# Keeping one step's split weights on chip between the two halves of an attention and gated-MLP layer, with key weights in two pieces and a new order

## The chip, the cores and the metric

The kernel runs on one core of one Trainium2 chip. The core has a matrix engine (TensorE, PE in the profile, with its weight loads as PEld), a vector engine (DVE), a scalar engine (ACT), a general engine (POOL) and SyncE (SP), which here only issues DMA transfers. The metric is the device time of one execution in microseconds. For the kernel before, three runs gave 565.55, 566.1 and 568.32 us; the median is 566.1.

## The reference

For x of 2048 tokens by 512, normalised to `xn` (layer norm without weights):

```python
qkv = xn @ wqkv                                   # 32 heads of 16
pq, pk = q @ w_phi, k @ w_phi                     # per head, 16 by 16
phi(p) = concat(softmax(p), softmax(-p))
kv = sum over tokens of phi_k^T v;  z = sum over tokens of phi_k
s = (phi_q kv / (phi_q z + 1e-6)) @ wo            # all tokens, no mask
h = (gate * (gate > 0)) * up;  gate = xn @ W_gate, up = xn @ W_up     # 512 x 1376 each
out = x + s * silu(h @ W_down)
```

All inputs and the output are fp32.

## The kernel before, in words

**Precision and tiles.** Every large product is made of three fp32r matmuls: each operand is split into a high part (a rounding copy on ACT) and a low part (the difference, on DVE or POOL). Gate and up are computed together with a scheme of seven products of sums of blocks (Winograd's) instead of eight, so that each step has seven groups of six matmuls. The hidden width of 1376 is padded to 11 steps of 128 (`NF` = 11, f = 0 to 10).

**Halves.** The tokens go in two halves of 1024. The first half is in one long list, `ORDER`: it loads and normalises all 16 token blocks, folds `w_phi` into the key and query weights, forms keys, values and queries and the sums `kv` and `z`, and then makes the 11 gate/up steps of the first half, most of its down products and the first three pairs of query blocks. Each name in `ORDER` is a small operation; `Plan.run` issues them in the order of the list, and each engine works off its own instructions in that order. The names used below:

- `ldN`, `bnN`, `pwN`, `biN`, `apN`, `TN`: load, statistics, root, shift, scaling and turning of token block N (tiles `xt`, `pxT`); `lcb` loads constants (`cb`), `lkN` a piece of the key weights (`wkT`), `FkN` folds a quarter of them on PE (`pfold`, two passes for each of four products); `pk` is the key product that follows.
- `rwF` loads the raw gate and up weights of step F (`rawg`, from `wf`), `rdF` the down weights (`rawd`). `fsF` and `ftF` form sums on POOL (`tab`). `faF`, `fbF`, `fcF`, `fdF`, `feF` are the rounding copies on ACT into `wa`, `wb`, `wc`, `wd`, `fd`, and `falF`, `fblF` and so on the differences on POOL.
- `putwaF` and the like store these split weights to DRAM (`ws`): nine transfers of 256 KB for a step, two each for `wa`, `wb`, `wc` and `fd` and one for `wd`.
- `gF.0` to `gF.6` are the seven products of step F on PE (`ga`, `seed`, `gc`, `gd`); `gtF`, `gmF`, `geF` and so on are their sums on ACT and DVE; `haF` to `hdF` split the result into `hh`.
- `dnCJI` is a down product on PE for chunk C of steps, half-block J and rows I (`py`), `dyCJI` adds it up (for the first chunk a copy on ACT, `y<-py`).
- `of_K` loads output weights (`wor`).

After the list, still in the first half, the last chunk of the down product, the SiLU, and the output product (`pso`) with the split attention result (`oh`, `ol`, in `o_split`, from `of`) follow. The second half is a loop over f in which `gate_up` uses weights that `f_reload` fetches from `ws`; part 0 brings `wa` and `wb`, part 1 `wc`, `wd` and `fd`. Its order on the engines is set when the program is built, by a planner with costs and due times (`Clock`) and by the order of the code.

**Order and buffers.** All loads and stores of SP go through one queue in the order of issue; an issue waits until the transfer eight before it has landed. Buffers come from pools with a fixed number: 24 of 4 KB for each partition (`u4`: a pair such as `wa`, `fd` or `hh`, or `oh`, `ol`), 14 of 2 KB (`u2`, among them `wd`). A tile that is made when no buffer is free waits for the last reader of an old one.

At the end of the first half the code fetches the weights of step 0 and, in the output products, the first part of step 1:

```python
        last_split()
        drain()
        if half == 0:
            f_reload(0, 0)
            f_reload(0, 1)
        fs = CHUNKS[-1]
```

All instructions that pass through `InOrder` carry its one line in the profile: 129 before, 132 after.

Of the kernel before, what the change touches and what calls it, by code (L numbers as in the profile page):

```python
# [42 lines left out]
td2 bi4 pw6 pk3.1 td4 sm0 bi6 sq2.1 ap4 pq1.1 pk2.3 ep7 pv0.1 sps1 tl1.0 sm1 sc0 T4 spill0 th2.0 pw7 sc1 st8 bi7
z0 sums2 ph0 mx2 th2.1 lo5 ap7 tl1.1 pl0 pk3.2 q1.0 pk3.3 q2.0 hS2 pv1.0 hi4 sh2 lo4 st10 pq1.0 ex2 mx3 ap6 P1.2
ep10 pv1.1 slo2 tl2.0 T6 sm2 pq2.0 pv0.2 th3.0 sh3 pv1.2 sc2 cS2 th3.1 tl2.1 ex3 hi6 P6.2 ph1 pv3.0 ep8 z1 pv2.0
sm3 tl3.0 tl3.1 pv1.3 pl1 cU2 pv3.1 pv2.1 sc3 T7 sq1.0 vh1 vl1 lo6 P7.2 st11 pw8 th4.0 th4.1 P5.2 z3 tl4.0 sums3
lpm pv3.2 cW2 pv0.3 aw2 hi7 tl4.1 hS3 bi8 ap8 lo7 vh0 P2.2 bankd P3.2 pw10 bi10 slo3 vl0 bankc st9 pv3.3 au2
bankb ap10 vh3 spill2 banka mx4 ep11 kv0 P4.2 ep9 pv2.2 pw9 ph3 vl3 sh4 st13 ex4 pl3 kv1 pv2.3 vh2 mx5 q3.0 ph2
z2 sh5 ex5 ep13 vl2 sm4 pw11 pq3.0 sm5 bi9 P1.3 pw13 kv3 pl2 cS3 sq1.1 vh4 T8 sc5 P6.3 spill3 ld12 ap9 sc4 hi8
z5 bi13 P3.3 cU3 lo8 bi11 T9 P7.3 kv2 sums4 ph5 cW3 P4.3 hi9 vl4 mx6 hS4 pl5 sh6 lo9 ph4 mx7 q3.1 spS2 spill1  # L50
slo4 sh7 z4 ex6 ap11 P1.4 pq3.1 vh5 sm6 cS4 P5.3 aw3 ex7 sm7 sc6 vl5 pl4 st15 P6.4 cU4 vh7 P3.4 P2.3 sc7 ap13
au3 P7.4 vl7 cW4 T10 T11 hi10 hi11 kv4 mx8 ph6 lo10 sums5 P4.4 kv5 st12 P5.4 ph7 z6 hS5 lo11 pl6 q4.0 ep12 sh8
aw4 mx9 ex8 pl7 ep15 P2.4 sh9 pw12 pq4.0 ld14 kv7 ex9 sq3.1 au4 vh6 P1.5 q4.1 bi12 sm8 slo5 vl6 ap12 sm9 cS5
P6.5 z7 st14 kv6 sc8 pq4.1 T12 sc9 cU5 T13 P7.5 hi12 z8 ph8 sums6 lo12 cW5 pl8 hS6 hi13 P3.5 slo6 vh8 ep14 mx10
P4.5 spS3 q5.0 lo13 q5.1 z9 ph9 pq5.0 pw14 P1.6 vl8 mx11 kv8 sh11 sh10 ex11 vh9 pq5.1 pw15 sm11 sq5.1 bi15 sc11
ex10 pl9 cS6 bi14 P5.5 rw0 sm10 sq4.0 P6.6 z11 ph11 P3.6 aw5 sc10 ap14 P2.5 vh11 ap15 mx12 T15 cU6 fd0 hi15 pl11
sq2.0 P7.6 vl9 sq3.0 cW6 au5 vl11 lo15 T14 kv9 sums7 kv11 sq5.0 sh12 ph10 hi14 P4.6 lo14 mx13 q6.1 vh10 z10 fdl0
ex12 pl10 P1.7 hS7 vl10 sh13 slo7 rd0 pq6.1 sm12 kv10 sc12 P5.6 fs0 cS7 ex13 P3.7 ph12 rw1 P6.7 aw6 fa1 ft0 cU7
fa0 sm13 fs1 sq4.1 sc13 mx14 P2.6 P7.7 rd1 q6.0 z13 cW7 vh13 ft1 sh14 fal1 fal0 fb0 putwd0 au6 pq6.0 vl13 P5.7
ph13 rw2 P4.7 ex14 aw7 pl13 vh15 mx15 rd2 q8.1 vh12 sm14 P2.7 pq8.1 sh15 sc14 kv13 fc0 q7.0 fb1 ex15 au7 sm15  # L60
vl12 fbl0 vl15 pl12 sq6.1 sq6.0 q8.0 sc15 ql0.1 ph15 pq7.0 g0.0 kv12 g0.1 sq8.1 pq8.0 qt0.1 fcl0 qm0.1 q7.1 pl15
rw3 vh14 z15 fe0 fd1 fbl1 ph14 gt0 qs0.1 g0.2 pl14 fe1 vl14 gm0 fdl1 kv15 pq7.1 g0.3 qe0.1 kv14 fc1 sq8.0 ka fa2
sq7.1 ge0 fel0 gf0 kb g0.4 g0.5 fs2 z14 g0.6 ft2 kp2 fb2 gp0 g1.0 ql2.0 fc2 ql0.0 fcl1 gt1 fs3 putwa0 kp3 qt0.0
z12 qm0.0 qs0.0 gs0 gn0 g1.1 ft3 gg0 g1.2 rd3 fd2 kt2 fel1 kp0 sq7.0 gm1 ge1 kt0 g1.3 kh2_ ha0 hc0 ql1.0 fa3
putwc0 gf1 g1.4 kh0_ kl0_ g1.5 kl2_ rw4 fbl2 fal2 qe0.0 g1.6 fb3 fc3 zp1 kt3 fcl2 qt2.0 g2.0 g2.1 gp1 qa0.0
ql1.1 zc1 fd3 gn1 putwd1 fdl2 rd4 zp0 gg1 hd0 g2.2 fs4 gs1 qm2.0 hb0 putwd2 kh3_ qs2.0 ha1 hb1 gt2 gm2 hc1
putwb1 zc0 g2.3 ge2 fbl3 qt1.1 gf2 putwb0 qm1.1 qa0.1 g2.4 kl3_ fal3 gp2 g2.5 ft4 kp1 g2.6 qs1.1 putwc1 rw5 kt1
kh1_ gn2 putwb2 dn010 g3.0 g3.1 qt1.0 kl1_ fdl3 hd1 qm1.0 putwa2 gt3 fcl3 gs2 dn013 g3.2 putwc3 putwa1 qw0.1 gm3
dy010 of_1 putfe0 putwb3 qb0.1 qw0.0 fc4 fcl4 putwa3 qe1.1 gg2 ge3 fd4 fb4 qs1.0 dn012 g3.3 qb0.0 gf3 fa4 dy012
fal4 fdl4 g3.4 putwc2 oh_1 dn000 dy000 g3.5 ql2.1 dn011 fs5 dy013 ha2 gp3 ft5 qr0 ow_1 g3.6 fe3 gs3 fd5 ha3 qd0  # L70
qn0.0 fbl4 qn0.1 qx0.10 dn002 fa5 dy011 qe2.0 fel3 g4.0 hb3 dn001 qx0.00 dy002 putwc4 qh0.10 gn3 rd5 qx0.11
qo0.10 gt4 putwd3 rw6 qw1.1 hb2 fdl5 qh0.11 qh0.00 qe1.0 qx0.01 qh0.01 g4.1 qo0.11 g4.2 dn003 os_1 qo0.00 gm4
qo0.01 g4.3 qk0.11 fal5 putwd4 dy001 qk0.00 rd6 ge4 fb5 dy003 gg3 putfe1 rw7 fc5 qw1.0 qa1.0 of_2 g4.4 qa1.1 hc3
fe2 putwa5 qk0.01 gf4 g4.5 fbl5 fel2 gp4 qc0.00 putwa4 qk0.10 qb1.1 g4.6 sf0 fs7 qc0.11 gs4 fcl5 qb1.0 dn110
putwd5 gn4 qr1 fd7 g5.0 rd7 dn113 qc0.10 g5.1 hd3 qt2.1 fd6 qd1 gg4 sg0 putwb4 sl0 dy113 hc2 gt5 putwc5 g5.2 hd2
qn1.0 gm5 qc0.01 dy110 ge5 dn112 fa6 fs6 rw8 putfe3 oh_2 g5.3 fa7 fal6 ft6 ft7 qn1.1 qz0.0 gf5 dn111 dy111 fb6
g5.4 dy112 gp5 qz0.1 fc6 qm2.1 g5.5 fb7 dn101 fbl6 qx1.00 fdl6 gs5 sw0 g5.6 fal7 dn100 qs2.1 putwb5 gn5 g6.0 gg5
ow_2 fe5 dy101 fcl6 qx1.10 dn102 fbl7 qh1.00 qx1.01 fe4 gt6 hc4 dy102 rd8 g6.1 putwb6 qh1.01 qh1.10 qo1.00 fdl7
dn103 hd4 qo1.01 gm6 putwa7 qe2.1 qo1.10 qx1.11 g6.2 qk1.01 ge6 fa8 fel4 qw2.1 g6.3 qh1.11 fel5 putwd7 qc1.01
sf1 g6.4 dy103 qw2.0 hc5 qa2.0 hd5 qk1.00 of_3 putwd6 g6.5 putwa6 qb2.1 putfe2 gf6 fc7 os_2 qo1.11 g6.6 qa2.1  # L80
putwc6 g7.0 fs8 gp6 ol0 qk1.11 sg1 putfe5 gs6 qc1.00 g7.1 fcl7 qc1.11 gt7 qb2.0 fe6 gn6 qk1.10 fal8 fel6 qc1.10
g7.2 putwb7 gm7 gg6 qr2 dn203 g7.3 ge7 fd8 oh_3 qd2 g7.4 rw9 gf7 ft8 qn2.0 putfe4 sl1 dy100 dn200 qn2.1 qz1.1
g7.5 gp7 gs7 dn202 rd9 fb8 putwc7 dy200 fe7 putwa8 qx2.00 qx2.11 ha4 fc8 fs9 fa9 g7.6 qh2.00 g8.0 ha5 fbl8 ow_3
dy203 gn7 gt8 g8.1 fdl8 g8.2 gm8 fcl8 dy202 g8.3 ge8 g8.4 qx2.10 ft9 sw1 qo2.00 rw10 fc9 gg7 g8.5 qx2.01 os_3
qh2.01 dn201 hb4 oa0 gf8 g8.6 fa10 fal9 fel7 qo2.01 qh2.10 qo2.10 gp8 qz1.0 fcl9 fb9 qk2.00 dy201 fd9 fbl9 g9.0
hb5 qh2.11 qo2.11 fs10 g9.1 qk2.11 qc2.00 g9.2 gt9 gn8 putwc8 fdl9 hc7 hc6 qk2.01 hd7 hd6 gs8 putwb9 gm9 of_0
ha6 qc2.11 fal10 putwa9 ge9 qk2.10 ft10 g9.3 qc2.01 g9.4 putwd8 dn211 gf9 oh_0 g9.5 dy211 dn210 qc2.10 ow_0
# [1433 lines left out]
```

## Time and profile before

| what | value |
|---|---|
| runs, us | 565.55, 566.1, 568.32 |
| profiled execution, own time | 568.91 us |
| its span, first to last instruction | 567.1 us |
| PE busy | 554.2 us (98%) |
| DVE, ACT, POOL busy | 415.0, 290.7, 423.5 us |
| moved by DMA | 136.14 MB, mean 240 GB/s |
| mean granted clock of TensorE | 0.996 |

The span is told from one profiled execution; the runs' times are of whole executions. A share of busy time is a mean over very different stages, so the stages are read one by one. In rows of instructions the columns are start, duration, engine, line, operation, tile written and tiles read, and in brackets how long the engine stood idle and what ended that.

### The profile page before, as it was taken

The numbers are of one execution on the slowest core, as the hardware profiler recorded it, in microseconds if no ns is written. First come the engines' busy times: TensorE is split into PE (matmuls) and PEld (weight loads), VectorE is DVE, ScalarE is ACT, GpSimd is POOL, SyncE is SP. The second block draws the span as 40 slices with busy tenths as digits, with TensorE's granted clock in tenths as the row PEclk, the third lists the DMA queues.
The fourth block names the chain that finished last, engine by engine and source line by source line (L and its number), as shares of the span: only waits on it lengthen the run. The fifth ranks groups of instructions, "written<-read, shape, count | busy, mean of one in ns | idle before, by whom it ended". The sixth has DMA issues, their size and how long they took to land.

```text
span 567.1 us, 8003 instructions
## 1 busy us (share of the span) xinstructions
PE 554.2 (98%) x2618; PEld 463.0 (82%) x2618; DVE 415.0 (73%) x621; ACT 290.7 (51%) x517; POOL 423.5 (75%) x325
## 2 busy tenths in 40 slices
PE   7999999999999999999899999999999999999997
PEld 6888888888888788878688887888888888888886
DVE  4998899889748899879664532599995959774322
ACT  4998887766565366445243232224563544534610
POOL 1798777688998898889886705553878888888476
PEclk8999999999999999999999999999999999999999
DMA  8646935375746888978999999996665766649883
GB/s 280 263 149 168 260 75 149 75 205 148 205 142 173 304 314 305 314 267 289 348 265 277 362 420 375 390 374 253 188 195 186 233 203 205 204 126 319 220 251 125
DMA packets 81562, 136.14 MB, mean 240 GB/s; under 512 B 7408, under 2 KB 34416, under 8 KB 80624
## 3 DMA queue, kind: packets, MB, share of 16 engines
q1 hardware_dynamic: 77920, 122.97, 63.2%
q0 software_dynamic: 3456, 12.58, 11.3%
q8 instruction: 21, 0.34, 0.3%
q14 instruction: 21, 0.17, 0.1%
q10 hardware_dynamic: 144, 0.07, 0.0%
HBM read 73.47 MB, written 53.74 MB: 224 GB/s over the span
## 4 chain that ended last, share of the span: by engine, by line
PE 86%; DMA 5%; POOL 4%; issue 2%; ACT 1%; DVE 1%; SPq 1%; ACTq 0%; POOLq 0%; DVEq 0%
PE py L129 17%; PE seed L129 9%; PE pd L129 8%; PE pa L129 8%; PE pso L129 8%; PE pq L129 8%; PE pc L129 5%; PE gc L129 4%; PE gd L129 3%; PE ga L129 3%; PE pkv L129 3%; PE pnum L129 2%; PE pk L129 2%; PE pv L129 2%; PE pfold L129 2%
## 5 line engine op out<-in xcount | busy, mean ns | idle before, releaser
L129 PE MATMUL py<-fd,hh 128*128 128x512 f32 x528 | 130.1, 389 | 0.0
L129 PEld LDWEIGHTS py<-fd,hh 128*128 128x128 f32 x528 | 99.0, 188 | 20.5
L129 DVE TENSOR_TENSOR y<-py,y 128x512 f32<-128x512 f32 x40 | 27.2, 687 | 32.1 <-PE py L129 32.1
L129 POOL TENSOR_TENSOR phl<-ek,phl 128x1024 fp32r<-128x1024 f32 x16 | 39.3, 2454 | 7.2 <-ACT phl L129 7.0
L129 PE MATMUL pso<-wo,oh 128*128 128x512 f32 (+1 forms) x136 | 39.8, 377 | 0.0
L129 POOL TENSOR_TENSOR ez<-eq,zB 128x1024 f32<-128x1024 f32 x16 | 38.5, 2415 | 1.1 <-PE py L129 1.1
L129 POOL TENSOR_TENSOR ol<-of,oh 128x1024 fp32r<-128x1024 f32 x8 | 19.1, 2399 | 25.8 <-issue 16.8
L129 PE MATMUL ga<-XT,wa 128*128 128x512 f32 x132 | 34.2, 394 | 0.0
L129 PE MATMUL pa<-XT,wa 128*128 128x512 f32 x132 | 33.7, 389 | 0.0
L129 PE MATMUL seed<-XT,wb 128*128 128x512 f32 x132 | 33.7, 390 | 0.0
L129 POOL TENSOR_TENSOR hh<-e,hh 128x512 fp32r<-128x512 f32 x11 | 14.3, 1296 | 25.7 <-ACT hh L129 25.7
L129 POOL TENSOR_TENSOR y<-y,ys 128x512 f32<-128x512 f32 x24 | 30.8, 1290 | 0.9 <-ACT ys L129 0.5
L129 DVE TENSOR_TENSOR y<-pso,y 128x512 f32<-128x512 f32 (+1 forms) x15 | 9.8, 656 | 29.2 <-PE pso L129 29.2
L129 PEld LDWEIGHTS ga<-XT,wa 128*128 128x128 f32 x132 | 24.5, 188 | 5.4 <-issue 0.5
L129 PEld LDWEIGHTS pa<-XT,wa 128*128 128x128 f32 x132 | 24.7, 188 | 5.1
L129 PEld LDWEIGHTS pso<-wo,oh 128*128 128x128 f32 x136 | 25.0, 188 | 4.7
L129 PEld LDWEIGHTS seed<-XT,wb 128*128 128x128 f32 x132 | 24.6, 188 | 5.0
L129 PE MATMUL pso<-wo,ol 128*128 128x512 f32 (+1 forms) x68 | 25.7, 378 | 1.2 <-POOL ol L129 1.2
L129 ACT ACTIVATE eq<-pnum 128x512 f32<-128x512 f32 x32 | 17.8, 592 | 15.8 <-PE pnum L129 15.8
L129 POOL TENSOR_TENSOR y<-y,sx 128x512 f32<-128x512 f32 x13 | 16.7, 1333 | 11.6 <-DMA sx<-x 10.5
L129 ACT ACTIVATE hh<-e 128x512 fp32r<-128x512 f32 x11 | 7.0, 633 | 33.6 <-DVE e L129 33.6
L129 POOL TENSOR_TENSOR pTl<-ez,pTh 128x1024 fp32r<-128x1024 f32 x10 | 24.1, 2406 | 0.0
(239 smaller groups left out, 1639.6 us busy)
## 6 DMA issues: line engine op xcount, KB each, us to landing
zacc<-ek POOLq DMA_DIRECT2D x16, 512.0 KB, 4.6
XT<-xts SPq DMA_DIRECT2D x7, 1024.0 KB, 14.5
rawg<-wf SPq DMA_DIRECT2D x11, 512.0 KB, 4.5
ws<-wa SPq DMA_DIRECT2D x22, 256.0 KB, 5.9
ws<-wc SPq DMA_DIRECT2D x22, 256.0 KB, 5.1
ws<-wb SPq DMA_DIRECT2D x22, 256.0 KB, 4.5
...
```

The lines of the kernel that those rows point to most:

```text
L129: return self.tc.keep_in_program_order(op(*a, **k))
```

## The change

Three things change.

1. Step 10 (`KEPT`) is not stored: `putwa10`, `putwb10`, `putwc10`, `putwd10` and `putfe10` go, and its split weights stay in their buffers. The second half takes the steps in the order 10, 0, 1, ..., 9 (`STEPS`), its down chunks are (10, 0), (1, 2), (3, 4), (5, 6), (7, 8, 9), and the reload of step 0 at the end of the first half goes; the one of the first part of step 1 in the output products becomes that of step 0. Nine stores and nine loads fewer.
2. The key weights are loaded in two pieces of 512 KB instead of four of 256 KB.
3. `ORDER` is a new list of the same operations, but for those that went.

```diff
+KEPT = NF - 1
+STEPS = [KEPT, *range(NF - 1)]
+CHUNKS_2 = [(10, 0), (1, 2), (3, 4), (5, 6), (7, 8, 9)]
 ORDER = """
-ld0 ld1 ld5 bn0 pw0 bn1 lcb lk0 st5 ap0 pw1 lk1 T0 bi1 Fk0 Fk1 ld2 ap1 T1 lk2 bn2 hi0 lo0 kh0 lk3 Fk2 kc0 lq0
+lcb ld1 bn1 pw1 lk0 ld0 Fk0 bi1 ap1 bn0 kh0 T1 Fk1 lk1 ld3 kl0 pw0 Fk2 lq0 ap0 hi1 lo1 kc0 lv0 kh1 Fk3 kc1 kc2
...
@@ prep_ops
                 if i is None and f in CHUNKS[-1]:
                     WD[f] = T[name]
+                elif i is not None and f == KEPT:
+                    FT.setdefault(f, [None] * 4)[i] = T[name]
...
+        if f == KEPT:
+            return
         for name, i in ((wa, 0), (wb, 2), (wc, 4), (fd, 7)):
             store(name, i, True)
@@ load_ops
-        for k in range(KD):
-            raw(f"lk{k}", "wkr", lambda: u8((P, KD, D), "wkT"), slice(k, k + 1), wkT[:, k:k + 1, :])
         for k in range(2):
+            raw(f"lk{k}", "wkr", lambda: u8((P, KD, D), "wkT"), slice(2 * k, 2 * k + 2), wkT[:, 2 * k:2 * k + 2, :])
@@ the halves
-        for f in range(NF) if half else ():
-            if f == 0:
+        for n, f in enumerate(STEPS if half else ()):
+            after = STEPS[n + 1] if n + 1 < NF else None
+            if n == 0:
                 queries = pace.add(all_queries(1), 5)
-            if f + 1 < NF and f + 1 not in FT:
-                f_reload(f + 1, 0)
+            if after is not None and after not in FT:
+                f_reload(after, 0)
...
-            run(gate_up(f, f > 1, lambda: f + 1 < NF and f_reload(f + 1, 1)))
-            for c, fs in enumerate(CHUNKS[:-1]):
+            run(gate_up(f, n > 1, lambda: after is not None and f_reload(after, 1)))
+            for c, fs in enumerate(CHUNKS_2[:-1]):
...
-        if half == 0:
-            f_reload(0, 0)
-            f_reload(0, 1)
-        fs = CHUNKS[-1]
+        fs = (CHUNKS_2 if half else CHUNKS)[-1]
...
-            HS.pop(g), WD.pop(g)
+            HS.pop(g)
+            if half or g != KEPT:
+                WD.pop(g)
...
             if half == 0 and m == 1:
-                f_reload(1, 0)
+                f_reload(STEPS[1], 0)
```

**The first instructions.** On SP, the first issues of the program before (`xt` are token blocks, `cb` the constants, `wkT` key weights):

```order
L129 DMA xt<-x 128x512 x3
L129 DMA cb<-cst 128x512
L129 DMA wkT<-wkT 128x512 x2
L129 DMA xt<-x 128x512
L129 DMA wkT<-wkT 128x512 x2
L129 DMA wqT<-wqT 128x1024
```

On SP after the change; the numbers at the end are the tile's shape, so `wkT` now moves 512 KB at a time, and one token block stands ahead of the key weights instead of three:

```order
L132 DMA cb<-cst 128x512
L132 DMA xt<-x 128x512
L132 DMA wkT<-wkT 128x1024
L132 DMA xt<-x 128x512
L132 DMA wkT<-wkT 128x1024
L132 DMA xt<-x 128x512
L132 DMA wqT<-wqT 128x1024
```

On PE before, behind the dummy products on `idle` (`pxT` turns a token block, `pfold` folds weights):

```order
L129 MATMUL pidle<-idle 128x128 x8
L129 MATMUL pxT<-ident,xt 128x128 x4
L129 MATMUL pfold<-cb,wkT 128x128 x8
L129 MATMUL pxT<-ident,xt 128x128 x4
L129 MATMUL pfold<-cb,wkT 128x128 x8
L129 MATMUL pk_304<-B11h,XT 128x512
```

On PE after the change; the first fold now stands ahead of the first turned block, and both turned blocks ahead of `pk`:

```order
L132 MATMUL pidle<-idle 128x128 x8
L132 MATMUL pfold<-cb,wkT 128x128 x4
L132 MATMUL pxT<-ident,xt 128x128 x4
L132 MATMUL pfold<-cb,wkT 128x128 x12
L132 MATMUL pxT<-ident,xt 128x128 x4
L132 MATMUL pk_302<-B11h,XT 128x512
```

**The first down products.** On ACT in the gate/up steps of the first half, around the first copies of down products (`y<-py`) before:

```order
L129 ACTIVATE XT<-pkb 128x2x64
L129 ACTIVATE t<-ga 128x512
L129 ACTIVATE y<-py 128x512
L129 ACTIVATE wc<-tab 128x512
L129 ACTIVATE eq<-eq 128x32x16 x2
L129 ACTIVATE wd<-rawg 128x256
L129 ACTIVATE wb<-tab 128x512
L129 ACTIVATE wa<-rawg 128x512
L129 ACTIVATE y<-py 128x512
L129 ACTIVATE woh<-wor 128x512
L129 ACTIVATE y<-py 128x512 x2
```

On ACT at the same place after the change. `wd<-rawg` is `fd6`, which reads the seventh load of gate weights; before it, `wd<-rawg` read the fifth, and one `y<-py` stood ahead of it; now two `y<-py` stand right behind it:

```order
L132 ACTIVATE t<-ga 128x512
L132 ACTIVATE wb<-tab 128x512
L132 ACTIVATE hh<-m 128x512
L132 ACTIVATE fd<-rawd 128x512
L132 ACTIVATE y<-py 128x512
L132 ACTIVATE eq<-eq 128x32x16 x2
L132 ACTIVATE wd<-rawg 128x256
L132 ACTIVATE y<-py 128x512 x2
L132 ACTIVATE sh<-sums 128x1024
L132 ACTIVATE wa<-rawg 128x512
```

On SP before, the rows that end in the seventh `rawg` load (`ws` are stores of split weights, `pql` query loads):

```order
L129 DMA ws_0_105<-wa 128x512
L129 DMA ws_1_106<-wa 128x512
L129 DMA ws_4_100<-wc 128x512
L129 DMA ws_5_101<-wc 128x512
L129 DMA pql<-pq_76 128x2x256
L129 DMA ws_4_118<-wc 128x512
L129 DMA ws_5_119<-wc 128x512
L129 DMA rawd<-wf 128x512
L129 DMA ws_6_111<-wd 128x512
L129 DMA rawg<-wf 128x1024
```

On SP after the change, the rows that end in it; a pair of output-weight loads (`wor`) and seven stores now stand close ahead:

```order
L132 DMA wor<-wo 64x1x512 x2
L132 DMA ws_6_120<-wd 128x512
L132 DMA ws_2_89<-wb 128x512
L132 DMA ws_3_90<-wb 128x512
L132 DMA rawd<-wf 128x512
L132 DMA ws_0_87<-wa 128x512
L132 DMA ws_1_88<-wa 128x512
L132 DMA ws_2_80<-wb 128x512
L132 DMA ws_3_81<-wb 128x512
L132 DMA rawg<-wf 128x1024
```

**The end of the first half.** On SP before, behind the reload of the operands of the second half (`XT`), the last of 20 stores and then the loads of step 0, ahead of the tokens `sx` for the output:

```order
L129 DMA ws_8_140<-fd 128x512
L129 DMA ws_0_168<-wa 128x512
L129 DMA ws_1_169<-wa 128x512
L129 DMA ws_7_148<-fd 128x512
L129 DMA ws_8_149<-fd 128x512
L129 DMA ws_6_174<-wd 128x512
L129 DMA ws_7_166<-fd 128x512
L129 DMA ws_8_167<-fd 128x512
L129 DMA wa<-ws_0_78 128x512
L129 DMA wa<-ws_1_79 128x512
L129 DMA wb<-ws_2_80 128x512
L129 DMA wb<-ws_3_81 128x512
```

On SP after the change, at the same place; no store and no load of weights stands between `XT` and `sx`, and step 0 comes behind the second `sx`:

```order
L132 DMA XT<-xts 128x2048 x7
L132 DMA sx<-x 128x512 x4
L132 DMA yk_177<-y 128x512
L132 DMA yk_178<-y 128x512
L132 DMA sx<-x 128x512 x2
L132 DMA wa<-ws_0_78 128x512
L132 DMA wa<-ws_1_79 128x512
L132 DMA wb<-ws_2_80 128x512
L132 DMA wb<-ws_3_81 128x512
L132 DMA out<-y 128x512 x6
```

More of the change, by code (lines that the diff above doesn't have):

```diff
@@ L43 @@
[L43 to L87, printed above, removed]
@@ new lines @@
+T0 kh2 lq1 bn3 hi0 kh3 ld2 pw3 lv1 pk1.0 kl1 Fq0 bi3 pk1.1 kc3 kl2 vh_0 ap3 qh0 ld5 Fq1 td1 pk1.2 sums0 Fq2 kl3
+vh_1 qh1 vl_0 ld4 lo0 vh_2 ld12 ql0 bn2 vl_1 qh2 ql1 pw2 T3 pk1.3 vl_2 hi3 lo3 st4 bi2 ap2 pk0.0 ld13 Fq3 qh3
+td3 pv1.0 pk0.1 ql2 st5 pk3.0 ld6 pv1.1 T2 ld11 hi2 mx1 ep4 pk0.2 pv1.2 sh1 th3.0 ql3 pk3.1 sps0 ld7 pw4 ep5
+vh_3 st7 pk0.3 lo2 bi4 ld9 pw5 tl3.0 sums1 ap4 vl_3 th1.0 ex1 q1.0 tl1.0 pv1.3 ep7 mx0 bi5 sh0 q1.1 pq1.0 ld8
+th1.1 ex0 st6 sm1 pw7 sm0 ep6 pq1.1 T4 vh1 td2 sc0 ap5 tl1.1 vl1 pw6 z0 pk3.2 sps1 q2.0 T5 bi7 sc1 hi4 pk2.0
@@ new lines @@
+sm4 sh5 P5.2 cS3 sc4 P3.3 aw2 sq3.0 ex5 ap9 st12 sm5 pl3 P6.3 spill2 ld14 z4 P2.2 sc5 pw10 T9 cU3 ap8 kv2 hi9
+au2 vh4 ph4 T8 P7.3 ep12 bi10 kv3 cW3 lo9 sums4 vl4 P5.3 hi8 hS4 mx6 P4.3 ph5 lo8 ap10 pl4 aw3 P2.3 slo4 st13
+kv4 sh6 mx7 au3 ex6 P1.4 sh7 vh5 pw12 z5 cS4 q3.1 sm6 ex7 pl5 sc6 ld15 st15 sm7 ep13 pq3.1 vl5 P6.4 cU4 ph6 P3.4
+T10 P7.4 hi10 pw13 sc7 lo10 T11 cW4 bi13 sums5 z6 mx8 hi11 kv5 P4.4 vh6 hS5 q4.1 pl6 lo11 ph7 vl6 mx9 ap13 z7
+bi12 q4.0 pq4.1 pl7 P5.4 sq2.1 sh8 sh9 kv6 ex8 slo5 sm8 pq4.0 aw4 P1.5 P2.4 ex9 ap12 ep15 sc8 vh7 cS5 ph8 P6.5
@@ new lines @@
+P3.5 sm9 z8 cU5 au4 T12 sc9 st14 spS2 pw15 hi12 mx10 vl7 pl8 P7.5 lpm T13 z9 vh9 cW5 ep14 kv7 lo12 sums6 vh8
+P4.5 vl8 bi15 ph9 hi13 q5.0 pl9 sh10 lo13 ex10 P5.5 mx11 hS6 kv8 sm10 pq5.0 aw5 vl9 pw14 sh11 sc10 vh11 P1.6
+slo6 spill3 cS6 spS3 ex11 P2.5 vl11 ph10 kv9 ap15 rw0 bi14 P6.6 au5 q5.1 z10 sm11 sq4.0 vh10 rd0 ap14 sc11 vl10
+pl10 cU6 fd0 T14 pq5.1 P7.6 sq5.1 T15 hi14 sums7 ph11 cW6 P3.6 hS7 sq5.0 kv10 z11 rw1 hi15 P4.6 pl11 lo14 lo15
+q6.1 slo7 fdl0 mx13 pq6.1 P1.7 mx12 sq3.1 P5.6 sh13 sq6.1 fs0 cS7 fs1 sh12 ex13 sq4.1 aw6 kv11 P6.7 rd1 sm13
@@ L93 @@
+putwa8 putfe7 hd7 g10.0 putwc9 gn9 dn313 qz2.1 putwb9 qz2.0 g10.1 ha8 fcl10 ow_0 fd10 gt10 wl1 dn303 gm10 fdl10
+g10.2 wl3 oa1 ge10 g10.3 dy303 hc8 ha9 gf10 hb8 ol2 os_2 hb9 g10.4 gg9 os_0 putfe6 putfe9 wl2 putfe8 ql3.1 gp10
+dn301 wl0 dy301 xrA11 gs10 g10.5 hc9 oa2 dn310 dy311 dy310 hd8 xrS2 xrA12 g10.6 dn312 gn10 xrS3 gg10 dy312 dn300
+fel10 xrS1 dy300 dy313 ha10 hd9 xrA22 xrS4 dn302 hb10 hc10 hd10 dy302
 """
```

46 lines of the change are left out of this document (36 added, 10 removed).

## The prediction

> **What bounds the kernel now.** I read the page's first lines, then the busy time by stretch, then who TensorE (PE) waited for, then the timelines at those places.
>
> ```profile
> span 567.1 us, 8003 instructions
> PE 554.2 (98%) x2618; PEld 463.0 (82%) x2618; DVE 415.0 (73%) x621; ACT 290.7 (51%) x517; POOL 423.5 (75%) x325
> ```
>
> PE is busy for 554.2 of 567.1 us and runs at full clock nearly throughout. Both programs list the same matmuls, so the change can win or lose only in the 12.9 us in which PE is not busy, and in its slow start. Where those are:
>
> ```profile
> core 0: us, PE busy (x) PEld busy (x) DVE busy (x) ACT busy (x) POOL busy (x), PEclk, DMA share, GB/s
> 0.00:10.00 10.00, 6.02 (x24) 4.78 (x25) 3.27 (x11) 4.00 (x7) 1.55 (x6) 1.00 0.77 224
> 10.00:20.00 10.00, 10.00 (x66) 9.56 (x66) 7.68 (x19) 7.40 (x14) 3.98 (x4) 0.83 1.03 409
> 190.00:200.00 10.00, 9.23 (x43) 7.38 (x42) 9.03 (x15) 1.08 (x4) 9.92 (x10) 1.00 0.95 327
> 250.00:260.00 10.00, 9.17 (x44) 7.29 (x43) 7.87 (x12) 7.20 (x13) 8.25 (x6) 1.00 0.47 163
> 280.00:290.00 10.00, 7.55 (x35) 5.96 (x34) 7.61 (x13) 3.90 (x8) 8.01 (x8) 1.00 1.05 312
> 340.00:350.00 10.00, 8.79 (x40) 6.92 (x39) 2.14 (x4) 4.09 (x6) 7.15 (x3) 1.00 1.03 395
> 560.00:567.10 7.10, 3.40 (x27) 3.12 (x25) 2.42 (x5) 0.00 (x0) 1.55 (x2) 0.95 0.40 149
> ```
>
> The missing time is 3.98 us in the first stretch, 0.77, 0.83, 2.45 and 1.21 us at four places, and 3.7 us in the tail, which the change leaves alone. The waits name them (total, times, longest):
>
> ```profile
> PE gc L129 <- DVE y L129: 3.2, 2, 2.5
> PE pfold L129 <- DMA wkT<-wkT: 2.5, 1, 2.5
> PE seed L129 <- DVE idle L129: 1.5, 1, 1.5
> PE pso L129 <- POOL ol L129: 1.2, 1, 1.2
> PE gd L129 <- DVE pTl L129: 0.8, 1, 0.8
> ```
>
> So the most that can be won inside the first half is 0.77 + 0.83 + 2.45 + 1.21 = 5.26 us, and at the start about 2.5 us of waiting and what a slow clock adds.
>
> **The start.** The first folds of the key weights wait for the first piece of them:
>
> ```profile
> 0.75 1.33 SPq L129 DMA_DIRECT2D xt<-x  x3
> 2.12 0.43 SPq L129 DMA_DIRECT2D cb<-cst  x1
> 2.59 7.06 DMA wkT<-wkT
> 6.67 0.60 PE L129 MATMUL pxT<-ident,xt 128*128 128x128 f32 x4
> 9.78 3.56 PE L129 MATMUL pfold<-cb,wkT 128*128 128x128 f32 x16 [2.52 <-DMA wkT<-wkT]
> 13.14 0.73 PE L129 MATMUL pxT<-ident,xt 128*128 128x128 f32 x4
> 13.71 1.95 PE L129 MATMUL pfold<-cb,wkT 128*128 128x128 f32 x16
> 15.42 0.48 PE L129 MATMUL pk<-B11h,XT 128*128 128x512 f32 x1
> ```
>
> The piece lands at 2.59 + 7.06 = 9.65 us, as the fifth 256 KB transfer in line: 1280 KB in 8.9 us after the first issue at 0.75, 144 KB/us. After the change the line is the constants, one block of tokens and 512 KB of key weights: 1024 KB, which at that pace land at 0.75 + 7.1 = 7.9 us. PE has its dummies, then the folds at 8.0 instead of 9.78. In both orders the first `pk` needs 32 fold passes; 4 transposes lie between them in the trace, 8 after the change, because the first token block is turned later. The first 16 passes took 3.36 us (9.78 to 13.14, 0.21 each) and the other 16 took 1.71 (13.71 to 15.42, 0.107 each). With the same 16 slow ones: 8.0 + 3.36 + 24 x 0.107 = 13.9 us, 1.5 earlier than 15.42. The second half of the key weights, 1792 KB into the line, is needed after 20 of these, at 8.0 + 3.36 + 4 x 0.107 = 11.8; at 144 KB/us it would come at 13.2, at the 409 GB/s of the second stretch from 7.9 on at 9.8. The middle is 11.5, so no wait is booked, but it could take 1.4 back. The token block that is turned after the first 8 passes, at 9.7, is the second in line instead of the first; the first one of the trace was turned at 6.67, and 256 KB more are 1.8 us: 8.5, in time. Bounds: 0 (weights no sooner, if these reads and not the bytes were slow) to -2.5 (the whole wait). I take -1.5.
>
> Why 16 passes run at half rate is not told by the wait: the clock of that stretch is 0.83, while the 2.45 us gap before `gc` at 281 us has 1.00 around it. The Trainium skill (TensorE: Matmul & The Clock Gate, "What's actually happening") says that a free-running window of about 3.4 us decides, half clock after an idle one. The trace agrees as far as it goes: two gaps of 2.5 us, one with slow matmuls behind it and one without. By that rule the new gap, from the last dummy to 8.0, may be short enough for full clock.
>
> **The four stalls.** The third, 2.45 us, can be followed:
>
> ```profile
> 266.73 0.93 SPq L129 DMA_DIRECT2D rawg<-wf  x1
> 273.30 0.63 ACT L129 ACTIVATE wa<-rawg 128x512 fp32r<-128x512 f32 x1 [3.07 <-DMA rawg<-wf]
> 277.99 0.60 ACT L129 ACTIVATE pTh<-pT 128x512 fp32r<-128x512 f32 x1 [4.05 <-POOL wd L129]
> 281.99 0.69 DVE L129 TENSOR_TENSOR m<-seed,t 128x512 f32<-128x512 f32 x1 [4.83 <-POOL hh L129]
> 283.93 1.67 PE L129 MATMUL gc<-XT,wc 128*128 128x512 f32 x6 [2.45 <-DVE y L129]
> ```
>
> A gate weight load issued at 266.73 holds ACT until 273.30; POOL's splits and ACT's copies queue behind, DVE's `m` waits 4.83 us for POOL, and PE waits for DVE. The first two stalls are shorter knots of the same engines. The new list moves every row there, so I cannot carry these three over one by one: each lies between staying (0) and going. DVE is idle for 1.0 to 2.4 us in each of those 10 us, so a better order has room, and nothing forces the stall. Of 0.77 + 0.83 + 2.45 = 4.05 I take two thirds as gone: -2.7 (0 to -4.05).
>
> The fourth is at the end of the first half:
>
> ```profile
> 336.56 1.04 ACT L129 ACTIVATE oh<-of 128x1024 fp32r<-128x1024 f32 x1
> 342.19 7.19 POOL L129 TENSOR_TENSOR ol<-of,oh 128x1024 fp32r<-128x1024 f32 x3 [14.56 <-issue]
> ```
>
> `oh` is ready at 337.60 and POOL has been idle, yet `ol` starts at 342.19, while the last `py` products run; PE's `pso` waits for it. What is missing is a buffer: before, the reload of step 0 has by then taken four new buffers of the 24 of 4 KB (`wa`, `wb`, `wc`, `fd`); the kept step needs three, and its `fd` is one that the last chunk holds anyway. With a buffer free, the first `ol` can follow `oh` and end at 337.6 + 2.4 = 340.0 (three of them took 7.19). PE got it at 342.19 + 2.4 = 344.6 after 1.2 us of waiting, so it wants it at 343.4. -1.21 (0 if it waits for another buffer).
>
> **The transfers saved.** Nine stores (2.25 MB) and nine loads (2.25 MB) of 256 KB go. They cost nothing now: they run under the last products and the output products of the first half, beside a busy PE:
>
> ```profile
> 320.00:330.00 10.00, 10.00 (x46) 8.29 (x45) 5.34 (x9) 3.85 (x6) 7.43 (x6) 1.00 1.03 367
> 330.00:340.00 10.00, 10.00 (x46) 8.29 (x45) 4.06 (x6) 3.48 (x5) 0.00 (x0) 1.00 1.01 419
> ```
>
> The queue is full there and PE is not short. In the second half step 10 starts on weights that are there; step 0 gets its last five tiles (`wc`, `wd`, `fd`) from the middle of step 10, as step 1 did from step 0, with no wait of PE in that place in the trace. The new pairs of the down product have the same sizes: 0.
>
> **What the new list adds.** On SP, between the sixth and the seventh gate load, stand sixteen stores, a down load and a pair of output-weight loads, and on ACT a copy from that very load (`wd<-rawg`) now stands ahead of two `y<-py` copies that free banks for PE's next `py`. The trace shows what such a load takes and what ACT's waits on weight loads came to:
>
> ```profile
> DMA to landing us min/median/max: 3.6/4.5/6.5
> ACT wa L129 <- DMA rawg<-wf: 4.6, 2, 3.1
> ACT fd L129 <- DMA rawd<-wf: 7.1, 1, 7.1
> 208.44 0.63 ACT L129 ACTIVATE woh<-wor 128x512 fp32r<-128x512 f32 x1 [2.40 <-DMA wor<-wo]
> ```
>
> The first row is of `rawg`. ACT stands in line for one fetched too late for up to 3.1 us, and PE would take that nearly in full, because the bank is wanted at once. Bounds 0 (landing by the median) to 3.1; I take the middle, +1.5.
>
> **Sum.** -1.5 - 2.7 - 1.2 + 1.5 = -3.9 us against the profiled execution, whose own time is 568.9 us (span 567.1). The median of the runs is 566.1, 2.8 lower, and PE's issue is the same in each: a part of the waits above is not in an ordinary run. I take -3.5 there: 566.1 - 3.5 = 562.6 us. Changes under 0.5% (2.8 us) can hardly be told from none for this kernel.
>
> **Rivals.**
> (a) The old stalls come back in other places, or the start wins nothing because the constants and key weights come slowly in any place. For it: three knots between 190 and 284 us, a crowded phase, with POOL busy for 9.92 of 10 us at the first. Against: the waits above are all that PE has in 567 us, so the engines have room. If the 2.7 booked as gone stays: 565.3; with nothing won at the start either, 566.8. Neither can be told from no change.
> (b) ACT's line for gate loads becomes the bound: the copy behind the seventh load waits as long as the longest such row, 7.1 us, and the knot of 283 us, of the same kind, stays. 566.1 - 1.5 - 0.77 - 0.83 - 1.21 + 7.1 = 568.9, slower. It decides once PE's wait there passes 7 us; against it is that the load's own longest landing is 6.5 and some of that runs before ACT gets to it.
> (c) The clock stays full through the first folds, as it did after the gap at 281 us. The 16 slow passes then cost 0.107 each, 40 of them end at 8.0 + 4.3 = 12.3 instead of 13.9; but the second key piece is wanted at 10.1, and where it comes at 11.5 the end is 13.6. So 0.3 to 1.6 more is won, 561.7 in the middle. This is what the Trainium skill's page named above, TensorE: Matmul & The Clock Gate, would give for a gap shorter than its window.
> (d) The part that names the change, the weights kept, does nothing: true of its transfers, by the rows above; only the buffer of the fourth stall ties it to the time. Without that 1.2: 563.8.
>
> **How the numbers follow.** Forecast with (c) as its lower edge 0.58 (0.15 of it for (c)), (a) and (d) together 0.33, (b) 0.09. The likeliest case alone reaches from 560.0 (everything won, little added) to 563.3. The range leaves out one in ten on either side: 559.8 to 567.0. Faster by over 0.5% is under 563.3: 0.58. Within: 0.33. Slower, over 568.9: 0.09.
>
> **What would show it.** The folds starting near 8.0 and the first `pk` near 13.9 us; no PE wait on `ol` and POOL's first `ol` right behind `oh`; PE's waits on DVE `y` under 1.5 us in all; a PE wait of 1 to 2 us on `py`, released by ACT, near 205 us, with ACT's wait on `rawg` ahead of it; equal PE time in the second half. Wrong would be: the folds still at 9.8; a wait on `py` of more than 4 us; new waits of PE between 20 and 190 us, where the order is new too and DVE has little room; a second half that is longer.

## The result, and the profile after

| | before | after |
|---|---|---|
| median of 13 runs each on one chip, us | 567.07 (565.16 to 568.66) | 563.77 (561.09 to 565.18) |
| profiled execution, own time, us | 568.91 | 564.09 |
| its span, us | 567.1 | 562.3 |
| moved by DMA, MB | 136.14 | 131.42 |

The ratio is 0.9942, with a 95% interval of 0.9923 to 0.9961: faster, by 3.3 us in the medians, 4.8 us between the two profiled spans. 562.6 was forecast. The sum fits; its parts fit less well.

The page of after, first the span and the busy time, then what PE waited for (total, times, longest, in us; these are all its waits in that list):

```profile
span 562.3 us, 7987 instructions
PE 554.1 (99%) x2618; PEld 462.8 (82%) x2618; DVE 414.5 (74%) x621; ACT 289.7 (52%) x517; POOL 423.6 (75%) x325
```

```profile
PE pfold L132 <- DMA wkT<-wkT: 2.7, 1, 2.7
PE seed L132 <- DVE idle L132: 1.5, 1, 1.5
```

PE is busy for as long as before (554.1 for 554.2 us). Of the five waits of before, the two at the start are left; the waits on DVE `y` and `pTl` and on POOL's `ol` are gone. By stretch (PE busy and its instructions first, the granted clock third from the end):

```profile
0.00:10.00 10.00, 5.83 (x25) 4.64 (x26) 2.75 (x9) 2.10 (x2) 0.77 (x5) 0.90 0.76 245
10.00:20.00 10.00, 10.00 (x61) 9.60 (x61) 7.48 (x17) 7.63 (x15) 4.74 (x4) 0.76 0.97 384
190.00:200.00 10.00, 9.92 (x45) 7.90 (x44) 9.79 (x17) 1.61 (x5) 9.18 (x9) 1.00 1.01 364
250.00:260.00 10.00, 10.00 (x50) 8.34 (x49) 8.14 (x13) 7.21 (x14) 9.25 (x10) 1.00 0.91 274
280.00:290.00 10.00, 10.00 (x46) 8.29 (x45) 9.96 (x17) 6.03 (x11) 9.58 (x11) 1.00 1.03 317
340.00:350.00 10.00, 10.00 (x46) 8.29 (x45) 2.65 (x4) 1.58 (x2) 6.05 (x4) 1.00 1.03 396
```

The four stretches with stalls are full now or nearly so (9.92 of 10 us in the first), but the first 20 us are worse: the clock is 0.90 and 0.76, where before it was 1.00 and 0.83, and 86 products are done in them instead of 90. PE's own rows show it:

```profile
3.33 2.51 PE L132 MATMUL pidle<-idle 128*128 128x128 f32 x16
8.56 2.04 PE L132 MATMUL pfold<-cb,wkT 128*128 128x128 f32 x8 [2.71 <-DMA wkT<-wkT]
11.24 4.51 PE L132 MATMUL pfold<-cb,wkT 128*128 128x128 f32 x24
15.95 0.48 PE L132 MATMUL pk<-B11h,XT 128*128 128x512 f32 x1
```

The first folds start 1.2 us sooner (8.56 for 9.78), yet the first `pk` comes 0.5 us later (15.95 for 15.42): 24 folds took 4.51 us here, 0.19 each, and 8 took 2.04, where 0.107 each was the full rate before; so most of them ran at half rate, some 24 of the 32, against 16 in the trace of before. (From start to start the 8 and the 24 take 1.83 and 4.36 us here; after_again, below, has them at full rate in 0.96 and 2.68. The 2.55 us more are 24 times 0.107.)

**The clock differs from execution to execution.** Each timed execution has its span and its mean granted clock. In the trace of before the slow stretch looks like this by windows of 3 us (the clock is third from the end):

```profile
10.00:13.00 3.00, 3.00 (x16) 3.00 (x16) 1.83 (x5) 1.08 (x2) 0.55 (x1) 0.50 1.03 414
13.00:16.00 3.00, 3.00 (x25) 2.91 (x25) 2.25 (x7) 2.32 (x5) 0.14 (x1) 0.93 1.04 416
```

That is 3 us at 0.50 and another 0.4 to make up 0.93: 3.4 us, which lower the mean over 567 us by 0.003. So 0.998 and more is counted as full clock here, and less as half. All executions of before that ran beside the experiments, and those of after in both its comparisons, as medians of the span:

| | full clock | half clock for some time |
|---|---|---|
| before, 83 executions | 563.5 us (54) | 565.9 us (29: 22 of 0.995 to 0.997 at 565.8, 7 lower still at 568.1) |
| after, 21 executions | 559.5 us (7) | 562.3 us (14: 12 at 562.1, 2 lower still at 562.8) |

At equal clock the change is worth 4.0 us, or 3.7 with one such stretch (565.8 and 562.1). One such stretch goes with 2.3 us more in before and 2.6 in after. That is more than its own price: 3.4 us at half rate lose 1.7 us. The rest is not explained here; in the traces of the new start, those where the clock fell also had the weights later (folds at 8.36 and 8.56 us, against 7.49 to 7.90 where it did not), so that sorting by clock sorts by the arrival of the weights as well. Both profiled executions, of before (0.996) and of after (0.993), were in the right column.

### The profile page after: what moved, and what is told of

Read it like the earlier page. It is cut to its first block, busy times and chain, and to the rows that moved or that the text cites. A ratio compares the mean times of both kernels' runs of the same rounds, so it can differ in the third digit from the quotient of the medians.

```text
span 562.3 us, 7987 instructions
## 1 busy us (share of the span) xinstructions
PE 554.1 (99%) x2618; PEld 462.8 (82%) x2618; DVE 414.5 (74%) x621; ACT 289.7 (52%) x517; POOL 423.6 (75%) x325
## 2 busy tenths in 40 slices
DMA packets 78682, 131.42 MB, mean 234 GB/s; under 512 B 7088, under 2 KB 34096, under 8 KB 77744
## 4 chain that ended last, share of the span: by engine, by line
PE 97%; DMA 1%; DVE 1%; ACT 0%; issue 0%; SPq 0%; DVEq 0%
PE py L132 21%; PE seed L132 9%; PE pa L132 8%; PE pd L132 8%; PE pq L132 8%; PE pso L132 8%; PE pc L132 5%; PE ga L132 5%; PE gc L132 5%; PE gd L132 5%; PE pnum L132 3%; PE pkv L132 3%; PE pk L132 2%; PE pv L132 2%; PE pfold L132 2%; PE pxT L132 1%
## 5 line engine op out<-in xcount | busy, mean ns | idle before, releaser
L132 POOL TENSOR_TENSOR phl<-ek,phl 128x1024 fp32r<-128x1024 f32 x16 | 40.9, 2559 | 3.0 <-ACT phl L132 3.0
```

The lines of the kernel that those rows point to most:

```text
L132: return self.tc.keep_in_program_order(op(*a, **k))
```

## The experiments

**keep_alone and order_alone: which part does it.** The first is before with the kept step alone, the second is after without it (the edits of the list told in words):

```diff
 keep_alone, against after
-ORDER: the new list, two key pieces
+ORDER: the old list without putwa10 putwb10 putwc10 putwd10 putfe10, four key pieces
 order_alone, against before
+ORDER: the new list, then putwd10 putwc10 putwb10 putwa10 putfe10; two key pieces
```

> The kernel before with the kept step alone: step 10 is neither stored nor fetched, the second half begins with it; four key pieces and the old list otherwise. Theory (the order of the list makes and removes the three mid-half stalls, the kept weights only free a buffer): PE still waits for DVE about 0.8, 0.8 and 2.5 us between 190 and 290 us, its wait of 1.2 us on ol is gone, and the time is 0.997 to 0.999 of before. Rival (the smaller traffic, 131.4 MB for 136.1, is what takes the stalls away): the three waits are gone here too and the ratio is 0.993 to 0.995.

Measured: 0.9966 (0.9937 to 0.9994), full-clock span 562.2 us (7 of 12 executions; 563.6 in the executions of before beside them). PE's waits, but for two of 0.3 and 0.2 us:

```profile
PE gc L131 <- DVE y L131: 2.8, 2, 1.9
PE pfold L131 <- DMA wkT<-wkT: 2.5, 1, 2.5
PE seed L131 <- DVE idle L131: 1.5, 1, 1.5
PE gd L131 <- DVE pTl L131: 0.8, 1, 0.8
```

The knots on DVE stay, 3.6 us in all, and the wait on `ol` is gone, as the theory has it. 4.7 MB less traffic takes none of the stalls on DVE away.

> The kernel after without the kept step: the new list and two key pieces, but step 10 is stored (its stores at the list's end) and the second half begins with step 0, fetched at the end of the first half as before. Theory: the three mid-half waits of PE (4.05 us before) are gone, since the list alone does that; the wait on ol, 1.2 us before, is back, since the four reloaded tiles take the buffers again; the start is that of after; ratio to before 0.994 to 0.997. Rival (the kept weights bring the gain): the mid-half waits are back in some measure and the ratio is 0.998 or more.

Measured: 0.9933 (0.9905 to 0.9960), full-clock span 560.2 us (7 of 12). Its waits behind the start, and POOL's first `ol`:

```profile
PE gc L128 <- DVE XT L128: 0.8, 1, 0.8
PE gc L128 <- DVE y L128: 0.4, 1, 0.4
PE pd L128 <- DMA wc<-ws: 0.3, 1, 0.3
```

```profile
333.80 4.78 POOL L128 TENSOR_TENSOR ol<-of,oh 128x1024 fp32r<-128x1024 f32 x2 [11.16 <-ACT oh L128]
```

The new list alone brings what the whole change does; the old knots are gone without the kept weights, though new ones of 1.2 us stand in their place. Which of the moves in the list undo the knots was not tested. One point of the theory missed: the wait on `ol` did not come back. With the new list `ol` follows `oh` at once even with step 0 reloaded and step 10 stored. What the kept weights add on top is 560.2 against 559.5 us at full clock, on different chips; that is too little to tell from nothing.

**reload_later: what `ol` waited for.** Before, with one edit:

```diff
-        if half == 0:
-            f_reload(0, 0)
-            f_reload(0, 1)
...
                 for q in QUERIES[half][:2]:
                     o_split(q)
+                if half == 0:
+                    f_reload(0, 0)
+                    f_reload(0, 1)
```

> The kernel before with one edit: at the end of the first half the reload of step 0 is issued behind the first two o_split instead of ahead of them. Theory (ol starts late because the reloaded tiles have taken the free buffers): POOL's first ol starts within 0.5 us of the end of ACT's oh, PE's wait of 1.2 us on ol at 343 us is gone, the time is 1.2 us shorter, ratio 0.998, if the reload, now later by four sx loads, is still in time for the second half. Rival (ol waits for some other buffer or reader): ol starts where it did, at 342, and the wait of 1.2 us stays.

Measured: 0.9978 (0.9950 to 1.0006). POOL's row in the trace, and PE's at the third knot:

```profile
335.73 4.76 POOL L129 TENSOR_TENSOR ol<-of,oh 128x1024 fp32r<-128x1024 f32 x2 [10.10 <-ACT oh L129]
```

```profile
277.66 0.61 PE L129 MATMUL gd<-XT,wc 128*128 128x512 f32 x2
280.35 2.47 PE L129 MATMUL gc<-XT,wc 128*128 128x512 f32 x6 [2.08 <-DVE y L129]
282.61 2.34 PE L129 MATMUL ga<-XT,wa 128*128 128x512 f32 x6
284.79 1.55 PE L129 MATMUL py<-fd,hh 128*128 128x512 f32 x6
```

`ol` starts at 335.73, straight behind `oh`, and PE has no wait on it: in the old list the reload's tiles had taken its buffer. The size fits too (1.2 us were expected, the full-clock span is 0.8 lower), though the interval holds 1. The second fence shows something else: a gap of 2.08 us in the middle of the kernel, and behind it two groups of six products in 2.47 and 2.34 us, where the next takes 1.55. In before a longer gap at the same place, 2.45 us, had full clock behind it (six products in 1.67 us).

**after_dummies and before_dummies: a start without a gap.** More products on `idle`, so that PE is busy until the key weights land:

```diff
-BY_VECTOR, IDLE = 4, 8
+BY_VECTOR, IDLE = 4, 16      # after_dummies; 18 in before_dummies
```

> The kernel after with 16 products on idle ahead of the folds in place of 8 of them, so that PE is busy until the first key piece lands near 8.4 us. Theory (the gap of 2.7 us before the folds, together with where the clock's windows fall, costs the 3.4 to 6.8 us at half clock that the start shows): the first pk stands at 13.6 us or earlier instead of 15.95, no stretch after 8 us shows half clock, and the time is 1.5 to 3 us under after, 0.989 to 0.992 of before. Rival (DVE, 96% busy from 20 to 50 us, sets the pace there): the first pk is as early, PE waits for DVE instead between 14 and 50 us, and the time is that of after, 0.994. Second rival: the clock falls to half at a fixed time after the start whatever PE does; the first pk stays at 15.4 to 16 us.

> The kernel before with 18 products on idle in place of 8, so that PE is busy until the first key piece lands; the old list otherwise. Theory (an idle gap is what brings half clock at the start, and it costs 2 us in some 4 of 10 executions): no execution under 0.998, all spans within 562.5 to 565, median 563.6, ratio 0.997 to 0.999, and the three mid-half waits stay as they are. Rival (with a full clock PE is only sooner at the stalls that follow and waits longer there): clock full, median not under 565, ratio 1.000.

Measured: after_dummies 0.9919 (0.9895 to 0.9943), before_dummies 0.9974 (0.9957 to 0.9990); all 24 executions had full clock. The folds and the first `pk`, after_dummies first:

```profile
8.43 1.06 PE L132 MATMUL pfold<-cb,wkT 128*128 128x128 f32 x8
12.79 0.48 PE L132 MATMUL pk<-B11h,XT 128*128 128x512 f32 x1
```

```profile
9.66 1.95 PE L129 MATMUL pfold<-cb,wkT 128*128 128x128 f32 x16
13.59 0.48 PE L129 MATMUL pk<-B11h,XT 128*128 128x512 f32 x1
```

That 24 of 24 stay at full clock with the gap filled, where 43 of 104 executions of before and after did not, says that the gap is what lets the clock fall. (The dummies themselves still begin slowly, though the profile gives the clock as 1.00 there: see the list at the end.) In before_dummies the other waits were `y` 1.2, `ol` 1.2 and `pTl` 0.8 us, so `y` came down to 1.2 from 3.2, where the expectation had the knots stay: they are not a fixed sum. In after_dummies the whole gain of the profiled start was lost again. Its span, 563.1 us, is its slowest execution; the median of its 12 spans is 560.3. The profiled one shows where:

```profile
PE py L132 <- ACT y L132: 1.8, 1, 1.8
PE gc L132 <- DVE XT L132: 1.1, 1, 1.1
PE gc L132 <- DVE y L132: 0.7, 2, 0.4
```

```profile
206.13 0.42 ACT L132 ACTIVATE wd<-rawg 128x256 fp32r<-128x256 f32 x1 [3.22 <-DMA rawg<-wf]
206.45 1.07 ACT L132 ACTIVATE y<-py 128x512 f32<-128x512 f32 x2
```

This is the wait of the prediction, PE on `py` behind ACT's copy of the seventh gate load. So neither theory held alone: the clock stays full in every execution, and a late load can take back what the profiled start won. The median of 560.3 is also no better than the 559.5 of after at full clock, on other chips: what the dummies bring is that no execution falls to half.

**after_again: is half clock likelier with the new start?** The kernel after, unchanged, on another chip.

> The kernel after, unchanged, beside the others on one chip; each execution's span is sorted by its mean granted clock. So far 12 of 13 executions of after had a clock under 0.998 (median span 562.0 us), against 15 of 35 of before (565.8; 563.6 at 0.999 and 1.000). Theory (the gap ahead of the folds makes half clock likelier, some 2 us each time): again 8 or more of 12 under 0.998, those about 1 to 2 us longer than the others, ratio to before 0.993 to 0.996. Rival (chance, or the chip: the other kernel with the same start showed 5 of 12): about 5 of 12, ratio 0.990 to 0.993.

Measured: 0.9921 (0.9892 to 0.9950), two of eight executions under 0.998 (562.7 and 562.8 us, the others 559.4 to 560.5). The rival held: 12 of 13 in the first comparison belongs to that chip or to chance, and nothing shows that the new start is colder than the old. In its trace the first `pk` is at 11.92, four microseconds sooner than in the first trace of after:

```profile
3.33 3.58 PE L132 MATMUL pidle<-idle 128*128 128x128 f32 x16
7.49 1.13 PE L132 MATMUL pfold<-cb,wkT 128*128 128x128 f32 x8 [0.57 <-DMA wkT<-wkT]
11.92 0.48 PE L132 MATMUL pk<-B11h,XT 128*128 128x512 f32 x1
```

```profile
PE gc L132 <- DVE XT L132: 0.9, 1, 0.9
PE gc L132 <- DVE y L132: 0.3, 1, 0.3
```

The gap ahead of the folds is 0.57 us for 2.71, half of it because the weights come 1.07 us sooner, half because the same 16 dummies take 3.58 us for 2.51. With PE earlier, 1.2 us of waits on DVE are there, which the late start of the first trace may have hidden; it is not the start alone, for early_load below has none of them with its first `pk` at 12.73.

**late_load, early_load and early_alone: the seventh gate load.** `rw6` is its load on SP:

```diff
 late_load, against after
-... putwb0 rw6 ... qw0.1 putwc3 ge3 sf1 ...
+... putwb0 putwc3 sf1 rw6 ... qw0.1 ge3 ...
 early_alone, against after (early_load: with IDLE = 16 as well)
-... kl0_ putwa1 ... putwb0 rw6 ...
+... kl0_ rw6 putwa1 ... putwb0 ...
```

> The kernel after with one pair of stores and a load (1 MB) moved ahead of that seventh load, so that it lands about 2.6 us later, near 208. Theory (the copy behind it has no margin in after: it ended 0.03 us before PE wanted the bank): PE waits 2 to 3 us on py, released by ACT, near 207 us; nothing later takes it back; the time is 2 to 2.5 us over after, 0.998 to 0.999 of before. Rival (a wait on ACT's line is taken back by the engines that PE waits for later): the wait is there, but the time is within 0.5 us of after.

> The kernel after with 16 products on idle as in after_dummies, and the seventh load of gate weights (rw6) issued ahead of the last four of the stores in front of it instead of behind them. Theory (that load holds ACT's copy ahead of two copies of down products, and lands at 205.5 to 206 us however early PE is): it lands 2.5 us earlier, near 203.5, PE's wait of 1.8 us on py at 207 is gone, and the span falls by up to 1.8 us against a profile of after_dummies, the median of runs by 0.5 to 1.5 us to 561 us, 0.989 to 0.992 of before. Rival (the stores that are moved back hold the splits, POOL's or DVE's line is as late): another wait of PE of 1 to 2 us stands between 190 and 215 us and the time stays at 562.

> The kernel after with the seventh gate load ahead of four stores, as in early_load, but 8 products on idle as in after. Theory (the load is just in time in most executions of after, late in some): no PE wait on py near 205 us, and ACT's copy of that load has no wait; the median lies 0 to 0.7 us under that of after, 0.991 to 0.993, with some executions at half clock again, 1 to 2 us longer than the rest. Rival (the products on idle made the whole difference of early_load): ratio as after, and a wait of ACT on rawg near 203 us.

Measured: late_load 1.0006 (0.9980 to 1.0031), the gain of the change all gone; early_load 0.9910 (0.9881 to 0.9939), early_alone 0.9940 (0.9918 to 0.9962). SP's issue of the load and ACT's copies in after_again, then the same in late_load with PE's rows:

```profile
196.99 0.64 SPq L132 DMA_DIRECT2D rawg<-wf  x1
202.91 0.42 ACT L132 ACTIVATE wd<-rawg 128x256 fp32r<-128x256 f32 x1 [1.13 <-DMA rawg<-wf]
```

```profile
199.55 0.46 SPq L131 DMA_DIRECT2D rawg<-wf  x1
207.56 0.42 ACT L131 ACTIVATE wd<-rawg 128x256 fp32r<-128x256 f32 x1 [5.47 <-DMA rawg<-wf]
202.98 1.52 PE L131 MATMUL gd<-XT,wc 128*128 128x512 f32 x6
208.51 2.93 PE L131 MATMUL py<-fd,hh 128*128 128x512 f32 x6 [4.02 <-ACT y L131]
211.24 1.85 PE L131 MATMUL gc<-XT,wc 128*128 128x512 f32 x6
```

The load is issued 2.56 us later, as meant, but takes 8.0 us to ACT's copy instead of 5.9, so PE waits 4.02 us, and then comes a stretch at half rate: 2.93 us for six products instead of 1.52, and the next six slow in part. Eleven of twelve executions had a clock under 0.998. The median is 5.8 us over that of after_again, where 2 to 2.5 were expected; the wait of 4.02 and the slow products, 1.41 + 0.33 us, come to 5.8. So the price of this late load is its wait and, behind it, the clock as well. The other way about, with the load early, ACT has no wait on it:

```profile
201.88 0.41 ACT L131 ACTIVATE wd<-rawg 128x256 fp32r<-128x256 f32 x1
```

That is early_alone; its full-clock median is 559.5 us, the same as that of after. The load was just in time there, and moving it buys no time, only room. Its ratio, 0.9940, is a little over the 0.991 to 0.993 of its theory. Beside the filled gap early_load's trace has no wait of PE behind the first `seed`, where that of after_dummies lost 1.8 us on `py`; its six spans have a median of 559.0 us against 560.3, on another chip, and by the ratios, 0.9910 and 0.9919, the two can't be told apart.

**key_alone and all_four: the key pieces.** Before with two pieces, and early_load with four and 12 products on `idle` (the names of the pieces in `ORDER` go with them):

```diff
 key_alone, against before
-            raw(f"lk{k}", ..., slice(k, k + 1), wkT[:, k:k + 1, :])              # four
+            raw(f"lk{k}", ..., slice(2 * k, 2 * k + 2), wkT[:, 2 * k:2 * k + 2, :])  # two
 all_four, against early_load: the reverse, and IDLE = 12
```

> The kernel before with two 512 KB key pieces in place of four of 256 KB, old list otherwise: ahead of the first folds now stand three token blocks, the constants and 512 KB. Theory (the folds start when the bytes ahead of them are in): the folds start 0.7 to 1.8 us later than the 8.4 to 9.8 us of the old head, the gap of PE before them grows, more executions than the 4 in 10 of before have a clock under 0.998, and the time is 1.001 to 1.004 of before. Rival (a fixed time for each load decides, not bytes): folds as before, ratio 1.000.

> The kernel after with four key pieces of 256 KB (the first two where the first 512 KB stood), the early seventh gate load, and 12 products on idle. Theory (the first folds need one 256 KB piece alone, 256 KB sooner than in after): the folds start at 6.6 to 7.6 us, the first pk at 11 to 11.8, clock full, span 557 to 558.5 us, ratio 0.986 to 0.990. Rival (the later pieces and the token block come no sooner, or DVE and POOL, nearly full from 20 to 180 us, cannot follow): PE waits in the first 20 us or near 190, span as early_load, 558.5 to 559.5, ratio 0.991.

Measured: key_alone 1.0043 (1.0026 to 1.0060), with ten of twelve executions at half clock; all_four 0.9909 (0.9883 to 0.9934), full clock, median span 558.6 us. Two pieces by themselves cost some 2.4 us. The profiled execution of key_alone, one of the two at full clock, has its folds at 8.90, inside the range of the old head, so a later start is not seen in it; what is seen in the twelve is that half clock comes more often. The clock is not all of it: among executions at half clock key_alone is still 1.1 us longer than before (566.4 and 565.3), and its two at full clock 1.9 (565.0 and 563.1). How much of this is later weights stays open. In after the pieces stand behind one token block instead of three, and its folds start at 7.49 to 8.56 us, against 8.37 to 9.78 with the old head and four pieces. In all_four the folds start at 7.65 us, the first `pk` is at 12.02:

```profile
3.33 4.49 PE L131 MATMUL pidle<-idle 128*128 128x128 f32 x24
7.65 1.06 PE L131 MATMUL pfold<-cb,wkT 128*128 128x128 f32 x8
12.02 0.47 PE L131 MATMUL pk<-B11h,XT 128*128 128x512 f32 x1
```

The folds stand straight behind the dummies, with no wait for weights: here the dummies set the start, so how early a 256 KB piece lands stays open. Its theory's 0.986 to 0.990 was missed; the rival's 0.991 came. The best two versions, early_load and all_four, are equal at 0.991.

## Why the prediction was right, and where it was not

**The start (-1.5).** The transfers came as forecast: folds at 8.0 were said, and the five traces with the new start and 8 products on `idle` have them at 8.56, 8.36, 7.49, 7.72 and 7.90. The term failed in the profiled pair, +0.5, at the words "with the same 16 slow ones". How many passes are slow belongs to the execution, not to the program: none of the 32 in after_again, 16 in the profile of before, some 24 in that of after. At full clock the first `pk` stands at 13.48 and 12.63 with the old start (keep_alone, reload_later) and at 11.92, 12.16 and 12.34 with the new one (after_again, late_load, early_alone): -0.9 by their means.

**The three mid-half stalls (-2.7 of 4.05).** Right in kind; order_alone shows that the list does it. Two thirds was a fair guess by luck: in the first trace all of them went, in after_again 1.2 us of other waits on DVE stand there, and with the old list itself the knots vary: 4.05 us in the trace of before, 3.5 to 3.7 in keep_alone, key_alone and reload_later, 2.0 in before_dummies. Why they vary stays open; a start at full clock is not enough, since keep_alone and key_alone have it too.

**The fourth stall (-1.2).** Right: after's first `ol` starts at 334.10, straight behind `oh` (ACT, at 332.98), and PE has no wait on it. The cause, a buffer, is shown for the old list by reload_later. That the kept weights free it, as rival (d) took for granted, is true only there; in the new list it is free without them.

**The new wait on ACT (+1.5).** Mis-sized: 0.2 in the trace of after, 0 in after_again. In after the copy of the seventh load let PE go with nothing to spare:

```profile
205.91 0.42 ACT L132 ACTIVATE wd<-rawg 128x256 fp32r<-128x256 f32 x1 [1.48 <-DMA rawg<-wf]
206.24 1.07 ACT L132 ACTIVATE y<-py 128x512 f32<-128x512 f32 x2
205.32 1.52 PE L132 MATMUL gd<-XT,wc 128*128 128x512 f32 x6
206.87 1.66 PE L132 MATMUL py<-fd,hh 128*128 128x512 f32 x6
```

The place was right, and so was the size of ACT's wait: 1.48 us, the middle that was taken between 0 and 3.1. The step that failed is the next one, that "PE would take that nearly in full, because the bank is wanted at once". Undisturbed, six products follow the six before them after 1.36 us, start to start. In after_again, order_alone, after, after_dummies and late_load ACT waited 1.13, 1.36, 1.48, 3.22 and 5.47 us for this load, and `py` came 0, 0.08, 0.19, 1.93 and 4.17 us later than that behind `gd`. The first 1.3 us of ACT's wait are free, and all of the rest reaches PE.

**The transfers saved and the second half (0).** Right: from the first `pso` product to the last it is 344.6 to 563.1 us before and 339.7 to 558.1 after, 218.5 and 218.4, and keep_alone, which has the saved transfers alone, keeps the stalls on DVE.

**The sum.** -3.9 was worked out; 4.0 and 3.7 were measured at equal clock, and 4.8 between the two profiled spans. In that pair the parts are all seen: +0.5 at the first `pk`, -4.05 for the stalls on DVE, -1.2 for `ol` and next to nothing for ACT, -4.75 together. So errors cancelled there: the start was 2.0 us worse than forecast, the stalls 1.35 better, and the wait on ACT, 1.5, did not come. At full clock the start is worth -0.9 and `ol` -1.2; for DVE the 1.2 us of after_again stand against 3.5 to 3.7 in three traces of the old list and 2.0 in the fourth. That makes -4.4 to -4.6, or -2.9, around the 4.0 measured. The step from the profiled execution to the runs (-3.9 to -3.5) took a part of the waits to be missing there; what is seen to differ between executions is the clock, with 2.3 us, and the knots on DVE. The runs gave -3.3 on one chip and -4.3 on another.

**The rivals.** (a) was seen in part, as those DVE waits. (b) did not occur, and late_load shows its price with the load only 2.6 us later. (c) happens in 7 of 21 executions; in after_again the first `pk` is then at 11.92 us, sooner than its 12.3 to 13.6, and the second key piece was not waited for. The rule cited for it, that a free-running window of about 3.4 us decides (the Trainium skill, TensorE: Matmul & The Clock Gate, "What's actually happening"), agrees with the traces in its chance element: 2.45 us of gap had full clock behind it, 2.08 at the same place in reload_later half; and of two gaps of 2.5 us at the start, that of before had half, that of keep_alone full. The table in that section of the Trainium skill has half clock after at least one idle window; here gaps shorter than that were enough.
